# A deep-cross kernel on one core: tail operand copies in one PSUM bank, bias sums in another bank and place, one weight load on another queue

## The chip, the cores and the metric

The kernel runs on one core of one Trainium2 chip. The metric is the time on the device in microseconds for one execution. The kernel before took 130.77 us (median of 5 runs, 130.53 to 131.61).

## What is computed

Six cross layers of a recommender network. Every layer multiplies the running activation by a square weight matrix, adds a bias, multiplies by the layer-zero input element by element, and adds the running activation:

```python
B, F, D, L = 4096, 26, 16, 6          # Din = F * D = 416
# x0: (4096, 416), ws: (6, 416, 416), bs: (6, 416), all bfloat16
def reference(x0, ws, bs):
    x = x0
    for l in range(ws.shape[0]):
        x = x0 * (x @ ws[l] + bs[l]) + x
    return x
```

Because each layer adds x0 times something to x, the result is x0 times a sum. The kernel keeps that sum, x @ W over all layers so far, in PSUM and never clears it within a batch block: the first layer's matmuls start it, the others add to it. The eviction of layer l adds to it a bias that is itself a running sum (one plus the biases of the layers 0 to l) and multiplies by x0.

## The kernel before

**Tiling.** The batch of 4096 rows is cut into four blocks of 1024 (the loop over `s`), and a block is worked through the six layers (the loop over `l`), 24 steps in all. Activations lie transposed, features on partitions. The 416 features are three chunks of 128 (`NC`) and a tail of 32. The three main chunks are two halves of 512 batch columns each. The tail's 32 features times 1024 columns are folded into four lanes of 32 partitions, 256 columns each. A tail operand (`x0t_sb`, `xt_sb`) holds the tail twice, in columns 0 to 255 with the lanes in order, and in columns 256 to 511 with the lanes exchanged in pairs.

**One step on the TensorE.** The first half of the main chunks (`step`, `chunk`, line 277 on: each is four matmuls on 32 output columns of the array, recorded under line 201), then the tail rows (lines 342 and 357, in two parts, `part` 0 and 1: the tail features' share of the main chunks, and of the tail itself, the latter with the corner weights `wc_sb`), then the main chunks' share of the tail (line 373), then the second half of the main chunks. The VectorE evicts the main chunks (line 446), the ScalarE (ACT) the tail (line 498), the GpSimd (POOL) multiplies the tail by x0 (line 188), and ACT makes the exchanged copy of the tail (line 475).

**The start, which the change touches.** The first 768 rows of block 0 come in untransposed (`xin_sb`, three loads of 256 rows), and the TensorE transposes them. The queues are set by hand, and each engine runs its program in the order written. In order:

- TensorE: a warm-up (`fill`, line 234), the transposes of the first 512 rows (line 240, into PSUM banks 3, 4, 6 and 0, 5, 7, as `IN_BANKS` at line 94 says), the main chunks of the first layer for k=0 and k=1. Ahead of k=2 (line 307) come the transposes of the third 256 rows (`third_input`, line 222, into banks 6, 7, 3), the transposed tail (`tail_inputs`, line 213, the two copies into banks 5 and 4), the bias sums (`bias_sums`, line 246, into bank 6, so that they wait for the copy out of that bank, `s_inD` 5), and then k=2. The tail rows wait (lines 323 to 339) for the third input's copies, for both copies of the tail operand (`s_te`, `s_te0`) and for the tail weights (`s_wt`, `s_wtp`). Part 1 waits for the copied bias sums (`s_cb`) and the corner weights (`s_wc`).
- VectorE: two memsets, four copies of transposed input (line 421), two of the third input (line 426), the second copy of the tail operand (line 428), then the evictions.
- ACT: loads, two copies of input (line 468), one of the third input (line 472), the first copy of the tail operand (line 479), the bias sums (line 481), then the loop.
- SP issues DMAs in the order of lines 113 to 129: two input loads and the first weights, the tail weights of lane 0 (line 116), a transposing load of the last 256 rows of block 0 (line 117), the weights of the other layers, the transposing loads of the other blocks.
- POOL: memset of ones, the load of the biases, the identity and the mask for the bias sums (lines 161 and 165), the tail weights of lane 2 (line 169), four loads of corner weights (line 173), then the loop. The identity (`s_set` 1) releases the first transposes.

The tail weights of the odd lanes 1 and 3 come on ACT's queue (line 464).

Of the kernel before, what the change touches and what calls it, by code (L numbers as in the profile page):

```python
# [11 lines left out]
def bass_standalone__dcn_v2_cross__recsys_kernel(  # L12
# [8 lines left out]
    NC = 3  # L21
# [11 lines left out]
    with ExitStack() as es:  # L33
# [40 lines left out]
        s_inT, s_inD, s_inA = sem("s_inT"), sem("s_inD"), sem("s_inA")  # L74
        s_tp, s_te, s_te0 = sem("s_tp"), sem("s_te"), sem("s_te0")
        s_ti, s_to, s_mb = sem("s_ti"), sem("s_to"), sem("s_mb")
# [35 lines left out]
        def _(sp):  # L112
            sp.dma_start(xin_sb[:, 0:2, :], x0_v[:, 0:2, :]).then_inc(s_xin[0], 16)
            sp.dma_start(w_sb[:, 0, 0, :], ws[0, 0:128, :]).then_inc(s_w0, 16)
            sp.dma_start(xin_sb[:, 4:6, :], x0_v[:, 4:6, :]).then_inc(s_xin[2], 16)
            load_wt(sp, 0, 0, 1, s_wt[0])
            sp.dma_start_transpose(x0T_sb[:, :, 768:SB], x0[768:SB, 0:DF]).then_inc(s_x0T[0], 16)
# [39 lines left out]
        def _(pool):  # L157
            pool.memset(ones_sb[:, :], 1.0).then_inc(s_ones, 1)
            pool.dma_start(bsa_sb[1:L + 1, :], bs[:, :]).then_inc(s_bs, 16)
            pool.wait_ge(s_ones, 1)  # L160
            pool.affine_select(
# [6 lines left out]
            ).then_inc(s_set, 1)  # L168
            load_wt(pool, 2, 0, 1, s_wtp)
            pool.wait_ge(s_zero, 1)  # L170
# [28 lines left out]
        def _(pe):  # L199
# [13 lines left out]
            def tail_inputs():  # L213
                for r in range(2):
                    for g in range(4):
                        for i in range(2):
                            j = 2 * (g ^ i) + r
                            src = xin_sb[:, j, DF:D] if j < 6 else xtl_sb[:, j - 6, :]
                            ins = tile_mm(ps[lane(g), 5 - i, r * 128:r * 128 + 128], src, ident[:, :], g, True)
                ins.then_inc(s_tp, 1)  # L220
# [25 lines left out]
            def bias_sums():  # L246
                pe.wait_ge(s_bs, 16)
                pe.wait_ge(s_zero, 2)
                pe.wait_ge(s_set, 2)
                pe.wait_ge(s_inD, 5)  # L250
                for c in range(NC + 1):
                    for q in range(4):
                        f0 = c * 128 + 32 * q if c < NC else DF
                        ins = tile_mm(ps[lane(q), 6, c * 8:c * 8 + L], bsa_sb[:, f0:f0 + 32], u_sb[:, :], q, True)
                ins.then_inc(s_cbp, 1)
# [10 lines left out]
            for s in range(NS):  # L266
                for l in range(L):
# [34 lines left out]
                    if n == 0:  # L302
                        pe.wait_ge(s_w0, 16)
                        for k in range(NC):
                            if k == 1:
                                pe.wait_ge(s_w[0], 16)
                            if k == 2:
                                third_input()
                                pe.wait_ge(s_xtl0, 16)
                                tail_inputs()  # L310
                                bias_sums()
                            before_a(k)
                            for m in range(NC):
                                step(m, 0, k)
                    else:
                        if s == 0:
                            pe.wait_ge(s_w[l], 16)
                        chunk(0, 0, before_a)
                        chunk(1, 0)
                        chunk(2, 0)  # L320

                    if n == 0:
                        pe.wait_ge(s_inD, 6)
                        pe.wait_ge(s_inA, 3)
                        pe.wait_ge(s_te, 1)
                        pe.wait_ge(s_te0, 1)
                    else:
# [6 lines left out]
                    if s == 0 and l < 2:  # L334
                        if l == 1:
                            pe.wait_ge(s_wc[1], 32)
                        pe.wait_ge(s_wt[l], (48, 64)[l])
                    if n == 0:
                        pe.wait_ge(s_wtp, 16)

# [7 lines left out]
                    for part in range(2):  # L348
                        if n == 0 and part == 1:
                            pe.wait_ge(s_cb, 1)  # L350
                            pe.wait_ge(s_wc[0], 32)
# [63 lines left out]
        def _(dve):  # L415
            dve.memset(wc_sb[:, :, :], 0.0).then_inc(s_zero, 1)
            dve.memset(bsa_sb[0:1, :], 1.0).then_inc(s_zero, 1)
            for i, (h, c) in enumerate(IN_ORDER):
                if c != 1:
                    dve.wait_ge(s_inT, i + 1)  # L420
                    dve.tensor_copy(  # L421
                        out=x0T_sb[:, c, h * 256:(h + 1) * 256], in_=psT[:, IN_BANKS[h][c], 0:256]
                    ).then_inc(s_inD, 1)
            for c in (0, 2):
                dve.wait_ge(s_inT, 2 * NC + c + 1)
                dve.tensor_copy(out=x0T_sb[:, c, 512:768], in_=ps[:, THIRD[c], 0:G]).then_inc(s_inD, 1)  # L426
            dve.wait_ge(s_tp, 1)
            dve.tensor_copy(out=x0t_sb[:, 0, G:2 * G], in_=ps[:, 4, 0:G]).then_inc(s_te0, 1)
            dve.wait_ge(s_cb, 1)
# [30 lines left out]
        def _(act):  # L460
# [12 lines left out]
            def swap_lanes(buf, done):  # L473
# [4 lines left out]
            act.wait_ge(s_tp, 1)  # L478
            act.activation(out=x0t_sb[:, 0, 0:G], in_=ps[:, 5, 0:G], func=ACTF.Copy).then_inc(s_te, 1)
            act.wait_ge(s_cbp, 1)  # L480
            act.activation(
                out=cb_sb[:, :, :],
                in_=ps[:, 6, 0:8 * (NC + 1)].rearrange("p (c e) -> p c e", e=8)[:, :, 0:L], func=ACTF.Copy,
            ).then_inc(s_cb, 1)
            act.wait_ge(s_cb, 1)
# [77 lines left out]
```

## Time and profile before

| what | value |
|---|---|
| median of 5 runs | 130.77 us |
| the profiled execution itself | 130.85 us |
| its span in the profile | 129.0 us |
| granted TensorE clock, mean | 0.997 |
| TensorE (PE) busy | 124.3 us, 96% |
| its weight loads (PEld) busy | 62.6 us, 49% |
| VectorE (DVE) busy | 100.3 us, 78% |
| ScalarE (ACT) busy | 71.4 us, 55% |
| GpSimd (POOL) busy | 22.8 us, 18% |

The span runs from the first recorded instruction to the last. What lies around it, 1.85 us in this execution, belongs to the execution's time as well. A line number names a line of the kernel; where a helper records the operation, all its uses have the helper's line, so that line 201 stands for all matmuls on 32 output columns and line 107 for all loads of tail weights. In a timeline each row gives the start, the time taken, engine, line, operation, what is written and read, the shape, how many instructions were put together, and in brackets how long the engine was idle before and what ended that. PE is the TensorE's matmuls, PEld its weight loads, which run beside them. The chain of waits is followed back from the last instruction to what released it at each step.

### The profile page before, as it was taken

The numbers are of one execution on the slowest core, as the hardware profiler recorded it, in microseconds if no ns is written. First come the engines' busy times: TensorE is split into PE (matmuls) and PEld (weight loads), VectorE is DVE, ScalarE is ACT, GpSimd is POOL, SyncE is SP. The second block draws the span as 40 slices with busy tenths as digits, with TensorE's granted clock in tenths as the row PEclk, the third lists the DMA queues.
The fourth block names the chain that finished last, engine by engine and source line by source line (L and its number), as shares of the span: only waits on it lengthen the run. The fifth ranks groups of instructions, "written<-read, shape, count | busy, mean of one in ns | idle before, by whom it ended". The sixth has DMA issues, their size and how long they took to land.

```text
span 129.0 us, 5407 instructions
## 1 busy us (share of the span) xinstructions
PE 124.3 (96%) x2448; PEld 62.6 (49%) x2448; DVE 100.3 (78%) x154; ACT 71.4 (55%) x164; POOL 22.8 (18%) x41
## 2 busy tenths in 40 slices
PE   7999999999999999999999999999999999999980
PEld 6654444444444445445445445445445445445450
DVE  2349779779779779779779779779779789789790
ACT  0627357377736456476746456475745555555680
POOL 7602102102102122012012022012012032022130
PEclk9999999999999999999999999999999999999998
DMA  3999999999008616000008943000009807000026
GB/s 111 306 276 308 130 184 88 217 151 190 0 10 142 128 41 228 0 5 0 5 0 167 103 151 119 5 0 5 0 0 97 178 0 264 5 0 5 3 83 187
DMA packets 32934, 12.54 MB, mean 97 GB/s; under 512 B 25338, under 2 KB 32912, under 8 KB 32912
## 3 DMA queue, kind: packets, MB, share of 16 engines
q1 hardware_dynamic: 31536, 11.49, 46.1%
q10 hardware_dynamic: 1184, 0.67, 1.7%
q8 instruction: 19, 0.31, 1.0%
q0 software_dynamic: 192, 0.05, 0.2%
q14 instruction: 3, 0.02, 0.1%
HBM read 2.90 MB, written 3.41 MB: 49 GB/s over the span
## 4 chain that ended last, share of the span: by engine, by line
PE 96%; DVE 1%; issue 0%; DVEq 0%
PE ps L201 84%; PE ps L342 10%; PE ps L240 1%; DVE o_sb L451 1%; PE ps L395 0%; DVE x0T_sb L426 0%; DVEq L33 0%; PE ps L357 0%
## 5 line engine op out<-in xcount | busy, mean ns | idle before, releaser
L446 DVE SCALAR_TENSOR_TENSOR xT_sb<-ps,cb_sb,x0T_sb 128x512 bf16<-128x512 f32 x120 | 80.9, 744 | 16.9 <-PE ps L342 16.9
L201 PE MATMUL ps<-xT_sb,w_sb 128*32 128x512 bf16 (+1 forms) x1680 | 89.0, 364 | 0.0
L201 PEld LDWEIGHTS ps<-xT_sb,w_sb 128*32 128x32 bf16 x1680 | 43.0, 97 | 38.7 <-issue 4.2
L475 ACT ACTIVATE xt_sb<-xt_sb 32x256 bf16<-32x256 bf16 x80 | 33.1, 414 | 16.6 <-POOL xt_sb L188 15.9
L498 ACT ACTIVATE t_sb<-ps,cb_sb 64x256 f32<-64x256 f32 x48 | 22.5, 469 | 30.5 <-PE ps L201 30.2
L188 POOL TENSOR_TENSOR xt_sb<-t_sb,x0t_sb 128x256 bf16<-128x256 f32 x20 | 13.4, 672 | 81.5 <-ACT t_sb L498 81.5
L201 PE MATMUL ps<-x0T_sb,w_sb 128*32 128x512 bf16 (+1 forms) x336 | 18.5, 365 | 0.0
L446 DVE SCALAR_TENSOR_TENSOR xo_sb<-ps,cb_sb,x0T_sb 128x512 bf16<-128x512 f32 x23 | 15.6, 745 | 3.4 <-PE ps L342 3.3
L342 PE MATMUL ps<-xt_sb,wt_sb 32*128 32x512 bf16 x80 | 12.2, 379 | 0.0
L201 PEld LDWEIGHTS ps<-x0T_sb,w_sb 128*32 128x32 bf16 x336 | 8.4, 97 | 7.6 <-issue 1.0
L511 ACT ACTIVATE x0t_sb<-x_sb 32x256 bf16<-32x256 bf16 x24 | 9.9, 413 | 0.4
L357 PE MATMUL ps<-xt_sb,wt_sb 32*128 32x512 bf16 x40 | 7.8, 385 | 0.0
L342 PE MATMUL ps<-xt_sb,wc_sb 32*128 32x256 bf16 x80 | 7.7, 268 | 0.0
L342 PEld LDWEIGHTS ps<-xt_sb,wt_sb 32*128 32x128 bf16 x80 | 2.3, 92 | 8.5 <-DVE xT_sb L446 8.5
L342 PEld LDWEIGHTS ps<-xt_sb,wc_sb 32*128 32x128 bf16 x80 | 4.0, 93 | 2.3
L188 POOL TENSOR_TENSOR xot_sb<-t_sb,x0t_sb 128x256 bf16<-128x256 f32 x4 | 2.7, 671 | 12.6 <-ACT t_sb L498 12.6
L201 PE MATMUL ps<-const-bfloat16-1.0 128*32 128x256 bf16 x56 | 3.2, 418 | 0.8 <-PEq L548 0.8
L421 DVE COPY x0T_sb<-ps 128x256 bf16<-128x256 bf16 x4 | 1.0, 292 | 2.9 <-PE ps L240 2.9
L468 ACT ACT_TABLE_LOAD x1 | 1.3, 1283 | 3.4 <-issue 3.4
L201 PEld LDWEIGHTS ps<-const-bfloat16-1.0 128*32 128x32 bf16 x56 | 2.3, 143 | 1.2 <-issue 0.8
L342 PE MATMUL ps<-x0t_sb,wt_sb 32*128 32x512 bf16 x16 | 2.4, 379 | 0.0
L173 POOL DMA_DIRECT2D wc_sb<-in_ws_dram x4 | 2.2, 555 | 0.0
(45 smaller groups left out, 28.8 us busy)
## 6 DMA issues: line engine op xcount, KB each, us to landing
out_dram<-o_sb SPq DMA_DIRECT2D x3, 832.0 KB, 4.1
w_sb<-in_ws_dram SPq DMA_DIRECT2D x5, 312.0 KB, 4.2
xin_sb<-in_x_dram SPq DMA_DIRECT2D x2, 208.0 KB, 3.5
out_dram<-o_sb SPq DMA_DIRECT2D x1, 256.0 KB, 2.3
xin_sb<-in_x_dram ACTq DMA_DIRECT2D x1, 208.0 KB, 3.3
w_sb<-in_ws_dram ACTq DMA_DIRECT2D x1, 208.0 KB, 3.7
out_dram<-o_sb SPq DMA_DIRECT2D x1, 208.0 KB, 2.3
out_dram<-o_sb ACTq DMA_DIRECT2D x1, 208.0 KB, 2.7
```

Of the source, the lines that this page charges most:

```text
L173: pool.dma_start(wc_sb[lane(g), a:b, 32 * g:32 * g + 32], ws[a:b, DF:D, DF:D].rearrange("l p n -> p l n")).then_inc(s_wc[i], 16)
L188: pool.tensor_tensor(out=dst, in0=t32_sb[:, n % 2, :], in1=x0t_sb[:, s, 0:G], op=ALU.mult).then_inc(s_xt, 1)
L201: return pe.matmul(dst, lhsT=lhsT, rhs=rhs, start=start, stop=True, skip_group_check=True, tile_position=(0, 32 * q),)
L240: ins = pe.transpose(out=psT[:, IN_BANKS[h][c], (j % 2) * 128:(j % 2 + 1) * 128], in_=xin_sb[:, j, c * 128:(c + 1) * 128], identity=ident[ ...
L342: return pe.matmul(dst, lhsT=lhsT, rhs=srct[lane(g), cols], start=l == 0 and start, stop=True, skip_group_check=True, tile_position=(32 * ...
L357: pe.matmul(ps[:, NC * h + 2, :], lhsT=wt_sb[lane(g), l, 0:128], rhs=srct[lane(g), :].rearrange("p (b r) -> p b r", b=2)[:, ::-1, :], star ...
L446: dve.scalar_tensor_tensor(out=dst, in0=ps[:, NC * half + c, :], scalar=cb_sb[:, c, l:l + 1], in1=x0T_sb[:, c, o:o + H], op0=ALU.add, op1= ...
L451: dve.tensor_copy(out=o_sb[:, j0 + 4:j0 + 8, 0:256], in_=psT[:, 4, :].rearrange("p (j d) -> p j d", d=256)).then_inc(s_oeD, 1)
L468: act.activation(out=x0T_sb[:, 1, h * 256:(h + 1) * 256], in_=psT[:, IN_BANKS[h][1], 0:256], func=ACTF.Copy).then_inc(s_inA, 1)
L475: ins = act.activation(out=buf[lane(g), G:2 * G], in_=buf[lane(g ^ 1), 0:G], func=ACTF.Copy)
L498: ins = act.activation(out=t32_sb[HALVES[h], n % 2, :], in_=tail(h), func=ACTF.Identity, bias=cb_sb[HALVES[h], NC, l:l + 1],)
L511: ins = act.activation(out=x0t_sb[lane(g), s + 1, swap * G:(swap + 1) * G], in_=x4_sb[96:128, s, r * G:(r + 1) * G], func=ACTF.Copy,)
```

## The change

Five things change, all in the first 10 us of the program. Nothing is added to or taken from what is computed.

- Both copies of the block's first tail operand are transposed into one PSUM bank, number 5, at columns 0 to 255 and 256 to 511. ACT copies them out in one instruction of 512 columns; the VectorE's copy and its semaphore `s_te0` go.
- The bias sums are computed before the third input's transposes instead of behind the tail's, and into bank 4, which the second copy of the tail no longer needs. Their wait for `s_inD` goes.
- The copy of the bias sums out of PSUM moves from ACT to the VectorE, ahead of its copies of the third input. The TensorE waits for it (`s_cb`) ahead of the tail rows' part 0 instead of part 1.
- The tail weights of lane 0 are loaded on POOL's queue instead of SP's, and those of lane 2, already there, are issued earlier: both now stand between the load of the biases and the identity.
- The counts waited for follow: 32 instead of 48 on `s_wt[0]`, 32 instead of 16 on `s_wtp`.

```diff
--- before.py
+++ after.py
@@ -72,7 +72,7 @@
         s_wt = [sem("s_wt%d" % i) for i in range(2)]
         s_x0T = [sem("s_x0T%d" % i) for i in range(NS)]
         s_inT, s_inD, s_inA = sem("s_inT"), sem("s_inD"), sem("s_inA")
-        s_tp, s_te, s_te0 = sem("s_tp"), sem("s_te"), sem("s_te0")
+        s_tp, s_te = sem("s_tp"), sem("s_te")
         s_ti, s_to, s_mb = sem("s_ti"), sem("s_to"), sem("s_mb")
         s_xa, s_xb = sem("s_xa"), sem("s_xb")
         s_a32, s_xaP = sem("s_a32"), sem("s_xaP")
@@ -113,7 +113,6 @@
             sp.dma_start(xin_sb[:, 0:2, :], x0_v[:, 0:2, :]).then_inc(s_xin[0], 16)
             sp.dma_start(w_sb[:, 0, 0, :], ws[0, 0:128, :]).then_inc(s_w0, 16)
             sp.dma_start(xin_sb[:, 4:6, :], x0_v[:, 4:6, :]).then_inc(s_xin[2], 16)
-            load_wt(sp, 0, 0, 1, s_wt[0])
             sp.dma_start_transpose(x0T_sb[:, :, 768:SB], x0[768:SB, 0:DF]).then_inc(s_x0T[0], 16)
             for l in range(1, L):
                 sp.dma_start(w_sb[:, l, :, :], wmain(l)).then_inc(s_w[l], 16)
@@ -157,6 +156,8 @@
         def _(pool):
             pool.memset(ones_sb[:, :], 1.0).then_inc(s_ones, 1)
             pool.dma_start(bsa_sb[1:L + 1, :], bs[:, :]).then_inc(s_bs, 16)
+            for g in (0, 2):
+                load_wt(pool, g, 0, 1, s_wtp)
             pool.wait_ge(s_ones, 1)
             pool.affine_select(
                 out=ident[:, :], in_=ones_sb[:, 0:128], pattern=[[-1, 128]],
@@ -166,7 +167,6 @@
                 out=u_sb[:, :], in_=ones_sb[0:L + 1, 0:L], pattern=[[1, L]],
                 compare_op=ALU.is_ge, fill=0.0, base=1, channel_multiplier=-1,
             ).then_inc(s_set, 1)
-            load_wt(pool, 2, 0, 1, s_wtp)
             pool.wait_ge(s_zero, 1)
             for i, (a, b) in enumerate(((0, 1), (1, L))):
                 for g in (1, 3):
@@ -216,7 +216,7 @@
                         for i in range(2):
                             j = 2 * (g ^ i) + r
                             src = xin_sb[:, j, DF:D] if j < 6 else xtl_sb[:, j - 6, :]
-                            ins = tile_mm(ps[lane(g), 5 - i, r * 128:r * 128 + 128], src, ident[:, :], g, True)
+                            ins = tile_mm(ps[lane(g), 5, i * G + r * 128:i * G + r * 128 + 128], src, ident[:, :], g, True)
                 ins.then_inc(s_tp, 1)
 
             def third_input():
@@ -247,11 +247,10 @@
                 pe.wait_ge(s_bs, 16)
                 pe.wait_ge(s_zero, 2)
                 pe.wait_ge(s_set, 2)
-                pe.wait_ge(s_inD, 5)
                 for c in range(NC + 1):
                     for q in range(4):
                         f0 = c * 128 + 32 * q if c < NC else DF
-                        ins = tile_mm(ps[lane(q), 6, c * 8:c * 8 + L], bsa_sb[:, f0:f0 + 32], u_sb[:, :], q, True)
+                        ins = tile_mm(ps[lane(q), 4, c * 8:c * 8 + L], bsa_sb[:, f0:f0 + 32], u_sb[:, :], q, True)
                 ins.then_inc(s_cbp, 1)
 
             def out_chunk(c):
@@ -305,10 +304,10 @@
                             if k == 1:
                                 pe.wait_ge(s_w[0], 16)
                             if k == 2:
+                                bias_sums()
                                 third_input()
                                 pe.wait_ge(s_xtl0, 16)
                                 tail_inputs()
-                                bias_sums()
                             before_a(k)
                             for m in range(NC):
                                 step(m, 0, k)
@@ -323,7 +322,7 @@
                         pe.wait_ge(s_inD, 6)
                         pe.wait_ge(s_inA, 3)
                         pe.wait_ge(s_te, 1)
-                        pe.wait_ge(s_te0, 1)
+                        pe.wait_ge(s_cb, 1)
                     else:
                         pe.wait_ge(s_xb, NC * n)
                         if l == 0:
@@ -334,9 +333,9 @@
                     if s == 0 and l < 2:
                         if l == 1:
                             pe.wait_ge(s_wc[1], 32)
-                        pe.wait_ge(s_wt[l], (48, 64)[l])
+                        pe.wait_ge(s_wt[l], (32, 64)[l])
                     if n == 0:
-                        pe.wait_ge(s_wtp, 16)
+                        pe.wait_ge(s_wtp, 32)
 
                     def row(g, dst, lhsT, cols, start):
                         return pe.matmul(
@@ -347,7 +346,6 @@
                     lo, hi = slice(0, G), slice(G, 2 * G)
                     for part in range(2):
                         if n == 0 and part == 1:
-                            pe.wait_ge(s_cb, 1)
                             pe.wait_ge(s_wc[0], 32)
                         for h in range(2):
                             g, wm = 2 * h, slice(part * 128, part * 128 + 128)
@@ -421,11 +419,13 @@
                     dve.tensor_copy(
                         out=x0T_sb[:, c, h * 256:(h + 1) * 256], in_=psT[:, IN_BANKS[h][c], 0:256]
                     ).then_inc(s_inD, 1)
+            dve.wait_ge(s_cbp, 1)
+            dve.tensor_copy(
+                out=cb_sb[:, :, :], in_=ps[:, 4, 0:8 * (NC + 1)].rearrange("p (c e) -> p c e", e=8)[:, :, 0:L],
+            ).then_inc(s_cb, 1)
             for c in (0, 2):
                 dve.wait_ge(s_inT, 2 * NC + c + 1)
                 dve.tensor_copy(out=x0T_sb[:, c, 512:768], in_=ps[:, THIRD[c], 0:G]).then_inc(s_inD, 1)
-            dve.wait_ge(s_tp, 1)
-            dve.tensor_copy(out=x0t_sb[:, 0, G:2 * G], in_=ps[:, 4, 0:G]).then_inc(s_te0, 1)
             dve.wait_ge(s_cb, 1)
             for s in range(NS):
                 for l in range(L):
@@ -476,12 +476,7 @@
                 ins.then_inc(done, 1)
 
             act.wait_ge(s_tp, 1)
-            act.activation(out=x0t_sb[:, 0, 0:G], in_=ps[:, 5, 0:G], func=ACTF.Copy).then_inc(s_te, 1)
-            act.wait_ge(s_cbp, 1)
-            act.activation(
-                out=cb_sb[:, :, :],
-                in_=ps[:, 6, 0:8 * (NC + 1)].rearrange("p (c e) -> p c e", e=8)[:, :, 0:L], func=ACTF.Copy,
-            ).then_inc(s_cb, 1)
+            act.activation(out=x0t_sb[:, 0, :], in_=ps[:, 5, :], func=ACTF.Copy).then_inc(s_te, 1)
             act.wait_ge(s_cb, 1)
             for s in range(NS):
                 for l in range(L):
```

## Prediction before the result was known

> **What bounds the kernel now.** I read four views, in this order: the page's busy rows and its chain of waits, that chain in order of time over the first 9 us, the timeline of each engine over the same stretch, and the groups of instructions by shape.
>
> The chain first. On the page it reads:
>
> ```profile
> PE 96%; DVE 1%; issue 0%; DVEq 0%
> ```
>
> The chain that ended last is the TensorE (PE) almost all the way. From about 9 us on it is nothing else: one layer of one batch block is a piece of 4.33 us at line 201 and about 0.55 us at lines 342 and 357, every 4.87 us, 24 times, with no other engine between. So what other engines, queues or DMAs do after 9 us is worth nothing as long as it stays covered, and a change that only touches the start shifts everything behind it by one amount: the shift of the first tail rows (lines 342 and 357). The only places where the chain leaves the TensorE are the start and the output at the end, and the diff touches only the start. The same chain in order of time (start us, us, what):
>
> ```profile
> 4.03 1.42 PE ps L240 x12
> 5.45 1.55 PE ps L201 x32
> 7.00 0.02 issue
> 7.02 0.44 DVE x0T_sb L426
> 7.46 0.14 issue
> 7.59 1.02 PE ps L201 x28
> 8.61 0.32 PE ps L342
> ```
>
> Here is the one hole: at 7.02 the chain goes over to the VectorE copy out of bank 6 (line 426), and the TensorE comes back 0.14 us after that copy's end. The timeline of the TensorE says which instruction waited:
>
> ```profile
> 6.68 0.56 PE L201 MATMUL ps<-ident,xin_sb 128*32 128x128 bf16 x27
> ...
> 7.19 0.22 PE L201 MATMUL ps<-ident,xin_sb 128*32 128x128 bf16 x1
> 7.59 0.26 PE L201 MATMUL ps<-u_sb,bsa_sb 7*32 7x6 bf16 x16 [0.18 <-DVE x0T_sb L426]
> 7.78 0.83 PE L201 MATMUL ps<-x0T_sb,w_sb 128*32 128x512 bf16 x12
> 8.54 0.38 PE L342 MATMUL ps<-x0t_sb,wt_sb 32*128 32x512 bf16 x1
> ```
>
> From 6.68 to 7.19 run the 24 matmuls of the third input and the 16 of the tail inputs, ten groups of four in 0.51 us, so 0.056 us a group. The next group could start at 7.24. The bias sums start at 7.59, because they write bank 6 and wait for its copy: 0.35 us lost. They take until 7.78 (0.19), the 12 matmuls of step k=2 until 8.54 (0.76), and then the tail rows run.
>
> **The change part by part.** I follow the first tail row, which starts at 8.54 now.
>
> Bias sums moved. They now come right after step k=1, in bank 4, whose copy (line 468) is over before k=1 begins. The wait for the copy of bank 6 is gone: -0.35. Their other waits are met: the biases are issued at 1.38 and land 3.8 later, at 5.2, and both GpSimd masks are done under 4 us. They start at 6.68, where the third input starts now, and push it back by their own length d. The trace shows them only after a stall. There the group takes 0.19 in all with the gap to the next instruction, 0.10 if only the starts of its 16 matmuls count (the last one starts at 7.69, close view of the same timeline). In the new place they follow 512-column matmuls that give the queue time to run ahead, so I take 0.14 between these ends. As they cost 0.19 where they stand now, step k=2 would start at 7.24 + d = 7.38 in place of 7.78, and the tail rows could start at 8.14, 0.40 earlier.
>
> Both tail copies in one bank. What is late next is the tail operand itself. The rows of ScalarE (ACT) and VectorE (DVE), now:
>
> ```profile
> 7.13 0.38 ACT L472 ACTIVATE x0T_sb<-ps 128x256 bf16<-128x256 f32 x1 [1.63 <-PE ps L201]
> 7.49 0.38 ACT L479 ACTIVATE x0t_sb<-ps 128x256 bf16<-128x256 f32 x1
> 7.92 0.19 ACT L481 ACTIVATE cb_sb<-ps 128x24 f32<-128x24 f32 x1
> ```
>
> ```profile
> 7.02 0.76 DVE L426 CAST x0T_sb<-ps 128x256 bf16<-128x256 f32 x2 [1.24 <-PE ps L201]
> 7.69 0.41 DVE L428 CAST x0t_sb<-ps 128x256 bf16<-128x256 f32 x1
> ```
>
> The two 256-column copies (0.38 on ACT, 0.41 on DVE) become one of 512 columns on ACT alone. The nearest row is that of the final copies, same engine, same types and columns:
>
> ```profile
> L519 ACT ACTIVATE o_sb<-ps 128x512 bf16<-128x512 f32 x3 | 1.8, 597 | 0.3 <-PE ps L201 0.3
> ```
>
> So 0.60; an upper end is 0.69, the one with a bias and an f32 output (line 491). ACT reaches it at 7.49 + d, since the copy before it waits for the third input, which moves by d. It ends at 8.09 + d. From a copy's end to the matmul that waited for it went 0.15 us in the hole above (the first copy of line 426, 425 ns long, ends at 7.44; the bias sums start at 7.59). The tail rows can start at 8.24 + d = 8.38, not at 8.14: a new stall of 0.24 takes the place of the old one of 0.35. Sum: 8.38 against 8.54 is -0.16. With both ends of d and of the copy, the gain lies between 0.02 (0.30 - 0.19 - 0.09) and 0.20 (0.30 - 0.10).
>
> Sums of the biases copied by VectorE. A new first copy, 24 columns, ahead of the two third-input copies: on ACT it took 0.19; on DVE at most the 0.29 of 256 columns (line 421), at least nothing that would matter. It can start near 7.0, while DVE idles now (1.24 us before line 426), and ends by 7.2 to 7.3; the third input's first chunk arrives at 7.02 + d = 7.16. So the two copies slip by up to 0.13, to an end of 7.78 + 0.14 + 0.13 = 8.05, and could release the tail rows at 8.20. The 8.38 of the tail operand hides that by 0.18; the same for the bias wait, which now stands ahead of the tail rows. VectorE's own next work, the first evictions at 9.31, waits for the tail rows. ACT loses its 0.19, which nobody waits for.
>
> Weights moved from SP to GpSimd (POOL). Its timeline now:
>
> ```profile
> 1.38 0.72 POOL L159 DMA_DIRECT2D bsa_sb<-in_bs_dram  x1 [0.27 <-issue]
> 2.19 0.32 POOL L161 TENSOR_SCALAR_AFFINE_SELECT ident<-ones_sb 128x128 bf16<-128x128 bf16 x1
> 2.44 0.18 POOL L165 TENSOR_SCALAR_AFFINE_SELECT u_sb<-ones_sb 7x6 bf16<-7x6 bf16 x1
> 2.57 0.60 POOL L107 DMA_DIRECT2D wt_sb<-in_ws_dram  x1
> 3.16 2.20 POOL L173 DMA_DIRECT2D wc_sb<-in_ws_dram  x4
> ```
>
> Two issues of 0.60 now stand ahead of the identity: it ends at 2.10 + 1.20 + 0.09 + 0.32 = 3.71. The first transposes start at 4.01, when the first input has landed (issued at 0.81, 3.1 later: 3.9), so the identity is still 0.16 early; at 0.72 an issue, as the biases took, it would be 0.08 late and cost that. The weights are issued at 2.1 and 2.7 and land 4.3 later, at 6.4 and 7.0; needed at 8.2. The four corner loads (line 173) start at 3.77 instead of 3.16; the first pair's second is issued at 4.29 and lands 3.9 later, at 8.2. Part 1 of the tail rows starts 0.23 after part 0, at 8.61, so it must have landed by 8.47: covered by 0.3, where 1.1 were before.
>
> SP's queue loses one issue: all behind it goes out 0.51 earlier (2.28 instead of 2.79), the transposing load first, then five weight loads, the other tail weights and later transposes. Nobody waits for any of them on the chain, so no gain. For a loss, that transposing load meets other transfers earlier: the third input stands ahead of it on the queue; the small loads on ACT's queue (landing at 6.3 and 7.1, needed at 7.0 and 8.2) have 0.7 and 1.1 us left. I take zero.
>
> A rule that speaks against this part: the Trainium skill's page "SBUF — State Buffer", in "Summary: rules for kernel authors", says not to put a DMA on the GpSimd queue beside VectorE work, because VectorE's two-port modes lock GpSimd out while it writes descriptors; its section on the bandwidth-pool intuition puts a 620 ns DMA at about 3100 ns so. The row first: the third corner issue now (4.16 to 4.78) lies across two VectorE copies (from 4.42, line 421) and took 0.62, the first two, beside none, 0.52 and 0.50. That is 0.12 of contention at most. The moved weight issues, 2.1 to 3.3, meet no VectorE work; the second corner issue (4.29) now meets those copies. By the row it lands 0.1 later, still covered; by the rule it would be blocked until those copies end at 5.78. The same page's "Who interferes with whom" exempts a copy outside the two-port modes with at most one SBUF input, which fits the row. I take the row.
>
> **The rivals.**
> 1. Exchange of stalls, as summed: -0.16, 130.6. For it: each duration has a row of its own shape.
> 2. The wide copy doesn't bind (TensorE frees the operand sooner than I think, or the bias sums cost little): up to -0.40, 130.4. Against it: the copy's 0.60 row.
> 3. The start slips: identity or corner weights late by 0.1 to 0.4. That eats the gain: 130.7 to 131.1. For it: both margins fall to 0.2 and 0.3.
> 4. Slower: the lock of the rule holds. Place: the second corner issue at 4.29, blocked until 5.78. Price: landing at 5.78 + 3.9 = 9.7, part 1 at 9.8 in place of 8.77, so +1.1: 131.9. It decides a measurable loss once that load lands after 9.3, that is, once the issue is held up by over 1.1 us. Against it: the 0.62 row.
> 5. The change doesn't speed up its step at all: the sum says nearly so, since 0.24 of the 0.35 comes back.
>
> **How the numbers follow.** The profiled execution took 130.85 us, of which 129.0 are the span; 130.85 - 0.16 = 130.69. It lay 0.08 above the median of the runs, 130.77, so I forecast 130.6 for the median; the likeliest case alone spans 130.55 to 130.75. Chances: case 1 (with 5) 0.68, case 2 0.09, case 3 0.15, case 4 0.08. About 0.5%, 0.65 us, is what can be told from no change. Cases 1 to 3 stay inside it but for scatter (the runs span 130.53 to 131.61): 0.01 of case 1 on each side, 0.02 of case 2 as faster, 0.02 of case 3 as slower, and all of case 4. Faster 0.03, same 0.86, slower 0.11. The range takes in cases 1 to 3 with a little scatter: 130.25 to 131.1.
>
> **What would show it.** Right: bias sums at 6.68 directly after the k=1 matmuls, no idle TensorE before them; an ACT copy of 128x512 of 0.60 ending near 8.23; a new TensorE gap ahead of line 342, released by that copy; first tail row at 8.38; spans of 4.87 per layer unchanged. Wrong: transposes starting after 4.05 (identity late); a gap ahead of the corner matmuls (corner weights late) or POOL issues of 1 us and more; no gap ahead of line 342 (case 2).

## The result, and the profile after

The changed kernel takes 131.72 us (median, 131.32 to 133.05). The kernel before, run beside it, takes 130.72 us. The ratio is 1.0077, 95% interval [1.0058, 1.0095]: about 1.0 us slower, outside the forecast range. Medians here are of all runs, while ratios leave out those over 1.5% above the fastest of the same kernel. The profiled execution took 132.18 us, 0.46 above the median; its span is 130.4 us instead of 129.0, so it shows more of a loss, 1.4 us. The line of engines in the page's chain of waits:

```profile
PE 95%; issue 1%; DVE 1%; DVEq 0%
```

"issue" was 0% before: time in which the engine waited for nothing that the profile shows. The same chain in order of time says where it lies (start us, us, what):

```profile
5.42 3.05 PE ps L201 x90
8.48 0.23 issue
8.71 0.37 PE ps L341
...
9.32 2.59 PE ps L201 x49
11.91 0.86 issue
12.78 0.39 PE ps L201
```

The first hole, 0.23 ahead of the tail rows, is the one that was forecast. The second, at 11.91, was not. The timeline of the TensorE (PE) around it, first in the kernel before, where 32 matmuls of layer 1 run without one, then in the changed kernel:

```profile
11.37 1.90 PE L201 MATMUL ps<-xT_sb,w_sb 128*32 128x512 bf16 x32
```

```profile
11.54 0.38 PE L201 MATMUL ps<-xT_sb,w_sb 128*32 128x512 bf16 x1
12.78 0.40 PE L201 MATMUL ps<-xT_sb,w_sb 128*32 128x512 bf16 x4 [0.86 <-issue]
```

In layer 1, the first matmul of a group of four runs at 11.54 and the second 1.24 us later; in the other groups they start 3 or 4 ns apart. There is no wait in the program between them. So 1.24 of the 1.41 us lost come from a stop that no semaphore explains, and 0.17 from the start (tail rows at 8.71 instead of 8.54).

What the TensorE lacked is its next instructions. One DMA queue of kind "instruction" (q8) has 19 packets of 16 KB, about one for each 256 of the TensorE's 4942 recorded instructions; no other engine has over 200 recorded. The page "Runtime: NRT & Kernel Launch" of the Trainium skill says the same in "Instruction fetch mechanics": instructions are refilled in blocks of 16 KiB, 256 instructions, through a DMA queue of the engine's own. The stop is ahead of the TensorE's 451st recorded instruction; another, in two kernels below, is ahead of the 706th, 255 later. The DMA view finds the first such packet by narrowing the window: in the kernel before it starts in the 20 ns from 7.74, in the changed one not until 10.19. The queues of the kernel before from 7.74 to 7.76, and of the changed one from 7.00 to 10.19 and from 10.19 to 10.21 (queue, packets, MB, share of 16 engines; a packet counts with its whole time where it starts, so that the share can be over 100%):

```profile
q8 instruction: 1, 0.02, 388.1%
q1 hardware_dynamic: 13, 0.01, 107.8%
```

```profile
q1 hardware_dynamic: 1512, 0.89, 112.6%
q0 software_dynamic: 96, 0.02, 4.1%
```

```profile
q8 instruction: 1, 0.02, 347.5%
q1 hardware_dynamic: 7, 0.01, 94.7%
```

While the block waits, SP's queue (q1) keeps the 16 DMA engines full, mostly with the weights of the later layers. The packet takes 1.1 us, ends at 11.32, and the TensorE goes on at 12.78, 1.46 after that. In the kernel before it ends at 8.99; with the same 1.46 the block is there at 10.45, and its first instruction is due at 11.4. That is a margin of about 0.9 us in a resource that I had not looked at.

The other rows that answer to those of before: ACT and the VectorE (DVE) at the start.

```profile
7.55 0.38 ACT L472 ACTIVATE x0T_sb<-ps 128x256 bf16<-128x256 f32 x1 [1.95 <-PE ps L201]
7.91 0.60 ACT L479 ACTIVATE x0t_sb<-ps 128x512 bf16<-128x512 f32 x1
```

```profile
7.24 0.18 DVE L423 COPY cb_sb<-ps 128x24 f32<-128x24 f32 x1 [1.48 <-PE ps L201]
7.44 0.76 DVE L428 CAST x0T_sb<-ps 128x256 bf16<-128x256 f32 x2
```

The wide copy takes the 0.60 that was forecast, and the tail rows wait for it: it ends at 8.51, the VectorE's copies at 8.19, and the last tail weights landed at 7.68. And the bias sums:

```profile
6.90 0.26 PE L201 MATMUL ps<-u_sb,bsa_sb 7*32 7x6 bf16 x16
7.09 0.57 PE L201 MATMUL ps<-ident,xin_sb 128*32 128x128 bf16 x27
```

The last group of k=1 starts at 6.59, so the next could start at 6.80 (0.216 a group). The bias sums start at 6.90, and the third input only at 7.09: the group costs 0.29, with 0.1 of idle on either side. The weight loads (PEld) show why. First the kernel before, where the third input follows k=1, then the changed one:

```profile
6.04 0.32 PEld L201 LDWEIGHTS ps<-x0T_sb,w_sb 128*32 128x32 bf16 x8
6.47 0.11 PEld L201 LDWEIGHTS ps<-ident,xin_sb 128*32 128x32 bf16 x4
```

```profile
5.94 0.53 PEld L201 LDWEIGHTS ps<-x0T_sb,w_sb 128*32 128x32 bf16 x12
6.90 0.17 PEld L201 LDWEIGHTS ps<-u_sb,bsa_sb 7*32 7x32 bf16 x16 [0.42 <-issue]
```

Before, the loads run 0.2 us ahead into the next group. With the bias sums next they stop for 0.42 us: the group has 7 rows where its neighbours have 128. The Trainium skill's page "TensorEngine Tiling (Array Packing)", "Key Properties", says that a change of tiling mode drains the TensorE. It spoke against this change, and I had not weighed it. That 7 rows among 128 are such a change is my reading; `changed_full_rows` below fits it.

### The profile page after: what moved, and what is told of

It is laid out like the page before. It is cut to its first block, busy times and chain, and to the rows that moved or that the text cites. A ratio compares the mean times of both kernels' runs of the same rounds, so it can differ in the third digit from the quotient of the medians.

```text
span 130.4 us, 5404 instructions
## 1 busy us (share of the span) xinstructions
PE 124.8 (96%) x2448; PEld 62.6 (48%) x2448; DVE 100.2 (77%) x154; ACT 71.4 (55%) x163; POOL 23.3 (18%) x42
## 4 chain that ended last, share of the span: by engine, by line
PE 95%; issue 1%; DVE 1%; DVEq 0%
PE ps L201 84%; PE ps L341 10%; PE ps L240 1%; DVE o_sb L451 1%; PE ps L393 0%; DVEq L33 0%; PE ps L355 0%
```

## The experiments

The theory after the result (A, later F): the stop is a late block of instructions, held up by SP's bulk loads. Its rivals: GpSimd's earlier loads hold it up (B), the TensorE's new order makes the loss whatever the queues do (C, E), or the stop is chance (D).

**The two parts apart.** `queue_alone` is the kernel before with

```diff
-            load_wt(sp, 0, 0, 1, s_wt[0])
...
             pool.dma_start(bsa_sb[1:L + 1, :], bs[:, :]).then_inc(s_bs, 16)
+            for g in (0, 2):
+                load_wt(pool, g, 0, 1, s_wtp)
...
-            load_wt(pool, 2, 0, 1, s_wtp)
```

(and the counts waited for). `banks_alone` is the changed kernel with these lines undone.

> The kernel before with the queue part of the change alone: lane 0's tail weights go from SP's queue to GpSimd's, ahead of the identity; PSUM banks, bias sums and copies as before. In the changed kernel the TensorE stops for 1.24 us inside a group of four matmuls of layer 1 (11.54 to 12.78), between two matmuls that no semaphore separates, and the instruction queue's first 16 KB packet of the program starts at 10.2 where it started at 7.7 before. Theory A (instructions late, because SP's queue runs 0.5 us ahead and puts its bulk in front of the instruction packet): the stop is here too, first instruction packet near 10, time 131.6 to 132.0. Theory B (instructions late because of GpSimd's earlier transfers): the same here. Theory C (the cause is the TensorE's own new order): no stop, 130.7. Theory D (the stop is chance of one execution, and the loss lies in the start): 130.7 to 130.9, no stop.

> The changed kernel with its queue part undone: lane 0's tail weights on SP's queue and lane 2's behind the masks as before; one bank for both tail copies, bias sums ahead of the third input, and the copies as changed. Theories A and B: no stop in layer 1; first tail row at 8.5 to 8.7, so 130.7 to 130.9. Theory C: stop stays, 131.7. Theory D: 131.5 if the loss lies in the start's new order.

`queue_alone`: 131.08 us, ratio 1.0005 [0.9981, 1.0029], no stop. `banks_alone`: 132.35, ratio 1.0084 [1.0055, 1.0113], with two stops in its profile, which is that of the longest of its six runs (132.88):

```profile
12.34 0.61 PE L201 MATMUL ps<-xT_sb,w_sb 128*32 128x512 bf16 x8 [0.50 <-issue]
```

```profile
19.98 0.40 PE L201 MATMUL ps<-xT_sb,w_sb 128*32 128x512 bf16 x3 [0.66 <-issue]
```

Both forecasts of A failed: the queue part alone costs nothing that can be told, the other part alone as much as the whole change. C named the right part, but the loss is still a stop without a wait, at block boundaries, so the TensorE's order had to act through the block.

**Which queue.** `sp_keeps_slot` adds to the changed kernel, in SP's old place,

```diff
+            sp.dma_start(
+                spare_sb[0:32, :], ws[0:1, DF:D, 0:256].rearrange("l p n -> p l n")
+            ).then_inc(s_spare, 16)
```

`lane0_on_act` has `for g in (1, 3, 0)` on ACT's queue (line 464 of before) and only lane 2 on GpSimd's, behind the masks.

> The changed kernel, with one addition: SP issues in the old place a load of the same 16 KB into a spare tile, so that all that stands behind it on SP's queue is issued at its old time, while GpSimd's queue stays as changed. Theory A (SP's bulk early): no stop, 130.7 to 131.0. Theory B (GpSimd's transfers): the stop stays, 131.7.

> The changed kernel, with lane 0's tail weights on ACT's queue behind lanes 1 and 3 and lane 2's behind the masks on GpSimd's queue as before: SP's queue runs 0.5 us ahead, GpSimd's is as before. Theory A: the stop is here, 131.6 to 132.0. Theory B: no stop, 130.7 to 131.0. ACT's activation table load goes back by 0.5 us, which could cost the start up to 0.3 in every theory.

`sp_keeps_slot`: 131.67, ratio 1.0025 [0.9997, 1.0053], runs from 130.25 to 133.09. Its profiled execution, at 132.43, has a stop of only 0.04 in layer 1 and one of 0.80 in layer 2. It is one of the five of 22 that the ratio leaves out as too long, so 1.0025 is too kind to this kernel: the medians of all runs, 131.67 and 131.05, are 0.5% apart. `lane0_on_act`: 132.38, ratio 1.0105 [1.0068, 1.0143], above what either theory forecast, with a stop of 0.49 in layer 1. So GpSimd's earlier loads are not needed for the stop (B falls). SP's half microsecond goes with a later packet (8.38 and 8.87 us without it, 9.89 and 10.20 with it, in the table below); that it also costs time is not shown, since `banks_alone` loses as much without it.

**The theory mended.** F: the block is asked for near the TensorE's 195th recorded instruction and queues behind what SP has issued by then. In the changed kernel that instruction lies inside the bias group, over which the TensorE can't run ahead. The first test adds one wait to the changed kernel's SP queue (`changed_hold_bulk`); the second leaves the TensorE of the kernel before untouched and only moves SP's bulk ahead (`before_bulk_first`):

```diff
             for l in range(1, L):
+                if l == 2:
+                    sp.wait_ge(s_te, 1)
                 sp.dma_start(w_sb[:, l, :, :], wmain(l)).then_inc(s_w[l], 16)
```

```diff
             for l in range(1, L):
                 sp.dma_start(w_sb[:, l, :, :], wmain(l)).then_inc(s_w[l], 16)
-                if l == 1:
-                    for g in range(4):
-                        load_wt(sp, g, 1, L, s_wt[1])
+            for g in range(4):
+                load_wt(sp, g, 1, L, s_wt[1])
```

> The changed kernel with one wait added on SP's queue: the weights of layers 2 to 5 and all behind them go out only when ACT has copied the tail operand (near 8.4 instead of 6.2). The first four runs left this theory. Theory F: the TensorE's next 16 KB block of instructions is asked for at about its 195th recorded instruction and waits behind the bulk weights that SP has issued by then. Over the six traces, the time from that instruction (6.68 before, 6.28 queue alone, 6.76 banks alone, 6.79 slot kept, 6.80 lane 0 on ACT, 6.91 changed) to the start of the block's packet (7.75, 7.96, 8.87, 8.38, 9.89, 10.20) is 1.1, 1.7, 2.1, 1.6, 3.1, 3.3, and it grows with the lead of SP's layer-2 weights over that instruction (0.0, 0.1, 0.0, 0.1, 0.6, 0.7). F expects here: first block packet before 8.6, no stop in layer 1, 130.5 to 131.0; a stop in layer 2 may remain, since the bulk then meets the second block. Rival E (the new order of the TensorE's own work makes the loss, whatever the queues do): 131.7 as the changed kernel.

> The kernel before with one thing moved on SP's queue: the four loads of tail weights for layers 1 to 5 (1.9 us of issue) go behind the weights of layers 2 to 5, so these bulk loads start near 4.75 instead of 6.7. TensorE order, banks and everything else as before. Theory F: first block packet at 9.5 or later, a stop of 1 us or more inside layer 1 between two matmuls without a wait, 131.8 to 133.5. Rival E: no stop, 130.7 to 131.1.

`changed_hold_bulk`: 131.37, ratio 1.0032 [1.0008, 1.0055], longer than forecast, though the packet comes at 8.53 and the profile has no stop. `before_bulk_first`: 132.31, ratio 1.0102 [1.0066, 1.0138]. Its timeline:

```profile
12.24 2.12 PE L200 MATMUL ps<-xT_sb,w_sb 128*32 128x512 bf16 x36 [0.79 <-issue]
15.33 0.37 PE L341 MATMUL ps<-xt_sb,wt_sb 32*128 32x512 bf16 x1 [0.96 <-DMA wt_sb<-in_ws_dram]
```

With the TensorE's order of before, the packet comes at 9.82 and the stop appears, ahead of the 451st recorded instruction again. That is the first matmul of layer 1 here, for which the program does wait, but its weights had landed at 8.62 and its input was evicted at 9.97. So bulk ahead of the block is enough to make the stop. The longer time proves nothing about it: the second gap (0.96) is for the tail weights that this edit put behind the bulk. They landed at 15.19, and the rows that need them start at 15.33 instead of 13.41, which alone makes up the 1.9 us by which the span is longer. The forecast time came out right by luck.

**The bias sums put back.** `bias_behind_tail` is `banks_alone` with

```diff
                             if k == 2:
-                                bias_sums()
                                 third_input()
                                 pe.wait_ge(s_xtl0, 16)
                                 tail_inputs()
+                                bias_sums()
```

and the VectorE's copy of the sums behind the third input's. `bias_behind_tail_hold` adds two waits for SP, `s_te` ahead of layer 2's weights and `s_xb` (3) ahead of layer 3's.

> The changed kernel with its queue part undone (as banks_alone) and the bias sums put back behind the tail inputs, still in bank 4 and without their wait; the VectorE copies the sums after the third input. The bias group cost 0.29 in the changed kernel (6.80 to 7.09, with 0.1 of idle on either side of it). Here the tail rows would start at 7.24 + 0.29 + 0.76 = 8.29, and the tail operand (no longer pushed back by the bias sums) is ready for them at 8.09 + 0.2 = 8.29. So the start gains 0.25 on the kernel before. Theory F: the third input comes at its old time, so the block request stays at its old place against SP's bulk: no stop more often than before, 130.6 to 130.9 against 131.0 on this chip. Rival E': the loss comes with the tail operand in one bank: 131.7.

> The same, with SP's bulk held back in two steps: the weights of layer 2 wait for the copied tail operand, those of layers 3 to 5 and the transposing loads behind them for the last eviction of layer 0 (near 13.2). Theory F: the first two block packets each start within 1.5 us of being asked for, no stop in layers 1 and 2, little scatter between runs, 130.2 to 130.6. Rival E': 131.7. If the transposing loads of the next batch block come too late for ACT's copies of it, a new wait appears near 25 us.

`bias_behind_tail`: 130.68, ratio 0.9983 [0.9964, 1.0001]. `bias_behind_tail_hold`: 130.56, ratio 0.9969 [0.9950, 0.9989], runs from 130.11 to 131.18: the one version faster than the kernel before beyond its interval. Its chain has neither hole:

```profile
5.42 3.04 PE ps L205 x82
8.46 0.32 PE ps L345
...
9.02 4.33 PE ps L205 x84
```

`bias_behind_tail` and `banks_alone` differ by the place of a group of 16 matmuls and of the copy of its sums. That is worth about 1.3 us between the ratios (0.9983 and 1.0084, each against the kernel before on its own chip), though the two issue layer 2's weights and start their 195th instruction within 0.05 us of each other. Some 0.2 to 0.3 us of it is the start: the group costs about 0.28 behind the tail inputs too (the ten groups from the third input on, 0.056 each, start at 6.81, and step k=2 at 7.66), but there it no longer pushes back the tail operand. Its copy ends at 8.22 here, at 8.36 in `banks_alone` and at 8.51 in the changed kernel. What also differs is that the weight loads run on to 6.60 into the third input here, and stop until 6.75 there; the packet starts at 7.93 instead of 8.87.

**Three more turns at the block.** `changed_full_rows` takes the bias operands to 128 rows; `changed_more_warmup` moves every block boundary by 112 instructions; `before_hold` and `changed_hold_two` put the one wait, or both, into the kernel before and the changed one.

```diff
-        bsa_sb = sb("bsa_sb", [L + 1, D])
-        u_sb = sb("u_sb", [L + 1, L])
+        bsa_sb = sb("bsa_sb", [128, D])
+        u_sb = sb("u_sb", [128, L])
```

```diff
-                    tile_mm(ps[lane(q), 7, 0:256], const[:, 0:32], const, q, True)
+                    tile_mm(ps[lane(q), 7, 0:128], const[:, 0:32], const[:, 0:128], q, True)
-            fill(14)
+            fill(28)
```

> The changed kernel with the bias sums' operands on all 128 rows (rows beyond the seventh are ones against zero weights, so the sums are the same). In the changed kernel the group uses 7 rows, and the weight loads stop for 0.42 us ahead of it (next one at 6.90), while in the kernel before, and with the bias sums behind the tail, the weight loads run on into the third input (6.47, 6.60). Theory F2: the TensorE cannot run ahead over a group with another number of rows; that is what made the bias group cost 0.29 and what made it ask for its next block of instructions (recorded instruction 195, inside that group) later, behind SP's bulk. F2 expects: weight loads run on into the bias group, the group costs 0.1 to 0.2, the stop in layer 1 is gone or under 0.4, 130.8 to 131.2. Rival G (the place of the bias sums matters for another reason, for instance the VectorE's copy): stop and 131.7 stay. GpSimd starts its first load 0.1 later here.

> The changed kernel with its warm-up in 28 rounds of 128 columns instead of 14 of 256: the same columns and about the same time, 112 more instructions, so every block boundary falls 112 instructions earlier in the program's work; queues untouched. Theory F: the first block is asked for during the first transposes (near 4.5), ahead of SP's bulk of 6.2 and later; its packet starts before 6.5 and no stop is at the old place. The second block is then asked for near 9 and falls into the bulk instead, needed near 14.6: a stop of 0 to 1 us there. 130.7 to 131.8. Rival E or G: the stop stays between the same two matmuls of layer 1.

> The kernel before with the one wait of changed_hold_bulk on SP's queue (weights of layers 2 to 5 and what follows only after the copied tail operand). Theory F: the kernel before has a stop in some of its executions too, which would make part of its scatter (130.3 to 132.0); with the hold its runs lie at 130.3 to 131.0, median 0.1 to 0.3 below the kernel before. If its scatter comes from the TensorE clock's first full grant (4.2 to 6.3 us over the nine traces) alone, nothing changes.

> The changed kernel with SP's bulk held back in two steps, as in bias_behind_tail_hold. changed_hold_bulk lost its stop in the profile and still measured 131.37. Theory F: the rest is a stop in layer 2 in part of the runs, from the second block; with two holds 130.7 to 131.1. If it is the start alone (tail rows later by the bias group's 0.29 less the old stall), 131.0 to 131.3.

`changed_full_rows`: 131.31, ratio 1.0040 [1.0021, 1.0059], just above its forecast. Its weight loads:

```profile
6.28 0.28 PEld L202 LDWEIGHTS ps<-u_sb,bsa_sb 128*32 128x32 bf16 x16 [0.20 <-DMA bsa_sb<-in_bs_dram]
6.47 0.12 PEld L202 LDWEIGHTS ps<-ident,xin_sb 128*32 128x32 bf16 x5
```

The loads run on from the bias sums into the third input, the group takes 0.10 instead of 0.29, the packet starts at 8.22 and there is no stop. But this execution began layer 0 half a microsecond earlier (4.86 against 5.35), so the packet's time alone proves less. A new wait of 0.49, for the corner weights, stands ahead of part 1 of the tail rows, since GpSimd's queue starts 0.29 later here; that would keep it above the kernel before.

`changed_more_warmup`: 132.03, ratio 1.0109 [1.0060, 1.0157], no better and above its forecast. Yet the stop is gone from its place, and the first packet comes at 5.52, as a boundary moved by 112 instructions must have it. The loss is now elsewhere:

```profile
7.71 0.59 PE L201 MATMUL ps<-ident,xin_sb 128*32 128x128 bf16 x27 [0.95 <-DMA xin_sb<-in_x_dram]
```

The third input lands late, beside the packet. That the packet delayed it fits the times, but was not tried by itself. I had expected a stop at the second block, and none came.

`before_hold`: 130.84, ratio 0.9999 [0.9978, 1.0020]; the scatter of the kernel before is not this stop. I had expected it to be narrower. `changed_hold_two`: 130.96, ratio 1.0010 [0.9986, 1.0033]: no loss can be told any more, with the TensorE's order, the banks and the GpSimd loads as changed. As only SP's waits were added, the loss comes from SP's bulk; that it reaches the TensorE by way of the blocks is what the profiles show.

The profiles of all kernels side by side (us; "stop" is the idle time without a wait):

| kernel | SP issues layer 2's weights | 195th instruction | block's packet | its end | stop |
|---|---|---|---|---|---|
| before | 6.71 | 6.68 | 7.75 | 8.99 | none |
| queue_alone | 6.22 | 6.28 | 7.96 | 9.34 | none |
| bias_behind_tail | 6.75 | 6.81 | 7.93 | 9.07 | none |
| bias_behind_tail_hold | 8.22 | 6.79 | 8.07 | 9.21 | none |
| before_hold | 7.87 | 6.66 | 7.66 | 8.78 | none |
| changed_hold_two | 7.95 | 6.32 | 8.14 | 9.43 | none |
| changed_hold_bulk | 8.82 | 7.19 | 8.53 | 9.80 | none |
| changed_more_warmup | 7.28 | 3.28 | 5.52 | 6.86 | none |
| changed_full_rows | 6.21 | 6.35 | 8.22 | 9.48 | none |
| sp_keeps_slot | 6.72 | 6.79 | 8.38 | 10.55 | 0.04; 0.80, layer 2 |
| banks_alone | 6.71 | 6.76 | 8.87 | 10.99 | 0.50; 0.66, layer 2 |
| before_bulk_first | 4.75 | 6.59 | 9.82 | 10.92 | 0.79 |
| lane0_on_act | 6.21 | 6.80 | 9.89 | 11.03 | 0.49 |
| changed | 6.21 | 6.91 | 10.20 | 11.32 | 0.86 |

Stops are in layer 1 where no other layer is named. Packets that end by 9.80 go with no stop there, one that ends at 10.55 with 0.04 us, and those that end from 10.92 on with 0.49 or more.

Each row is one execution. The order of time in it hides that weight loads can run ahead. In `bias_behind_tail` they reach the first group behind step k=1 at 6.60, before SP issues layer 2's weights at 6.75; in `banks_alone` they reach the group at that place, the bias sums, at 6.75, after SP's 6.71. If the block is asked for there, it comes ahead of the bulk in the one and behind it in the other, which would explain what the place of the bias sums does. No run moved this order by itself, and `changed_full_rows` (6.28 after 6.21, no stop) does not quite fit.

## Why the prediction was wrong

The bound was read rightly, and so was the exchange of stalls at the start, its mechanism though not its size. I said "what other engines, queues or DMAs do after 9 us is worth nothing as long as it stays covered". That holds; I had left out one cover.

- **The term d of the bias sums was mis-sized.** I took 0.14 "as they follow 512-column matmuls that give the queue time to run ahead"; they cost 0.29, more than my upper end of 0.19, because the TensorE does not run ahead into a group of 7 rows.
- **The release of the tail rows took 0.21 instead of 0.15** (copy ends at 8.505, rows at 8.711; 0.20 to 0.33 in all ten kernels with the wide copy). With the 0.15 of d, and the end of step k=1 0.12 later in this execution (6.59 instead of 6.47, its first group took 0.37 instead of 0.23), 8.38 becomes 8.71. The 0.12 is chance of one execution. The other two take 0.21, and so the whole forecast gain of 0.16.
- **The step that failed: "a change that only touches the start shifts everything behind it by one amount: the shift of the first tail rows".** The tail rows moved by 0.17 us, and layer 1 then by a further 1.24. What the sum lacked is the arrival of the TensorE's own instructions. I counted who waits for SP's loads and which loads meet others ("I take zero"), and did not count the instruction blocks among the transfers. They meet the bulk on the same DMA engines, have no semaphore in the program, and show only as "issue" once they are late. None of my five rivals named it; most of the loss of 1.0 us is theirs, as `changed_hold_two` shows (1.0010 against 1.0077).
- **The zero for the queue part held by itself** (`queue_alone`, 1.0005). What brings the loss, also without the queue part, is the new place of the bias sums with the copy of them (`banks_alone` at 1.0084 against `bias_behind_tail` at 0.9983).
- **What held:** the 0.60 of the wide copy, which binds the tail rows as forecast; the VectorE's copy of the sums (0.18) hidden; the identity, done at 3.55 against 3.71 forecast, released nothing late. The corner weights were in time by luck: the second landed at 8.71, half a microsecond later than forecast, and only because the tail rows were late too (part 1 at 8.93 instead of 8.61) did nothing wait for it.
- **The slower rival, the lock on GpSimd, was wrong.** The changed kernel's second corner issue (4.16) lies across a VectorE copy (from 4.39) and takes 0.50; no issue grew. The third takes 0.62 as before, so what I had put down to contention is its own length.

**What stays open.** `banks_alone` and `sp_keeps_slot` issue SP's bulk at the same times, and their packets start 0.5 us apart (8.87, 8.38) and their ratios lie at 1.0084 and 1.0025; with 6 and 22 runs, five of them left out, this is not settled. `changed_hold_bulk` still loses 0.3%. Its profiled span is 129.5 us instead of 129.0, all of it from the start (tail rows at 9.00 instead of 8.54): its first two groups took 0.40 and 0.43 instead of 0.23 and 0.22, and the trace's record of the full TensorE clock begins at 6.26 instead of 5.38. That is one execution. Stops at the second block in other runs would fit as well, as its packet ends at 16.40, 1.8 us ahead of its use where a stopped TensorE took 1.3 to 1.6, but no trace of that kernel shows one. How the DMA engines order a block against other loads is read only from its start times: in `changed_hold_two` and `changed_more_warmup` the packet starts 1.8 and 2.2 us after the 195th instruction, though no weights of layer 2 or later had been issued by that instruction.

## What to carry to other kernels

When an engine runs a long unrolled program, its next instructions are a transfer like any other, with a due time: before putting bulk loads out earlier, or delaying that engine, look at when its instruction packets start and how long before their use. An idle stretch that ends in "issue" between two instructions without a wait, some 256 instructions apart, is their mark. Bulk that is not due for many microseconds can be held back on its queue by a wait on a semaphore that exists anyway, and a small group with another number of rows than its neighbours belongs where nothing that others wait for stands right behind it.

## What the runs showed of the hardware that was not expected

- Stops stand ahead of the TensorE's 451st and 706th recorded instructions. If a block is asked for 256 instructions ahead of its use, at the 195th, it had some 4.7 us here (6.68 to 11.37 in the kernel before); no trace shows the asking. It took from 1.0 to 3.3 us after the 195th instruction's start until the packet began, 1.1 to 2.2 us for the packet, and 1.3 to 1.6 us from its end to the first instruction of a stopped TensorE (11.32 to 12.78 changed; 10.99 to 12.34 and 18.41 to 19.98 `banks_alone`; 11.03 to 12.37 `lane0_on_act`).
- SP's own issue stalls where a block is served early. In the kernel before, SP's load of layer 4's weights takes 1.65 us to issue (7.74 to 9.38) while the packet runs from 7.75 to 8.99. In the changed kernel, whose packet comes only at 10.20, it takes 0.49. Four other traces have such a long issue beside an early packet, of 0.89 to 1.50 us (`before_hold`, `changed_hold_bulk`, `bias_behind_tail`, `changed_more_warmup`).
- A group of 16 matmuls with 7 rows among groups with 128 costs 0.29 us, the same group on 128 rows 0.10.
